# Attention and a gated feed-forward layer on one core: fewer, longer out-projection bursts in the loop, and a reordered first batch

## The chip, the core and the metric

The kernel runs on one core of a Trainium2 chip. The metric is the device time of one execution, in microseconds (us); lower is better. "Time" below is the median over executions; "span" is what the profiler saw between the first and the last instruction of one profiled execution.

Names used below: TensorE (PE) does matmuls, VectorE (DVE) and ScalarE (ACT) do elementwise work, GpSimd (POOL) does masks in the loop and issues loads. PSUM is where matmuls write. A "step" is one batch of the loop. A "pair" is two attention heads; there are four pairs (0 to 3) per batch.

## The reference

```python
# B, H, S, Nb, D = 8, 8, 576, 16, 64;  d_model = 512, d_ff = 1536
k_all = np.concatenate([beacon_k, k], axis=2)
v_all = np.concatenate([beacon_v, v], axis=2)
scores = q @ k_all.T / sqrt(D)             # causal mask; beacons always seen
a = softmax(scores)
x = (a @ v_all) as 4608 tokens x 512
out = (gelu(x @ w_gate) * (x @ w_val)) @ w_out
```

The output is 4608 x 512, float32.

## The kernel before

Scores are computed transposed, in four chunks per pair (widths 512, 480, 464 and 208 columns for each of two heads). Each chunk goes through two rotating PSUM buffers, then ScalarE's exp. A chunk therefore cannot start until the exp of the chunk two before it has been read. `ab(m)` issues chunks 0 and 1 of pair m, `cd(m)` chunks 2 and 3. `av(m)` ("attend") multiplies the exponentials by v, which gives x, and by a block of ones, which gives the denominators z. Both land in one PSUM tile `x_ps`, of which there is a single buffer; then `normalize` forms x / z. `o(n)` issues n out-projection matmuls of the batch before, which fill TensorE's time while ScalarE works. After the pairs come twelve gate/value tiles, whose first needs pair 3's product last.

```python
def normalize(b, m, by_act=False):
    ...
    if by_act:                                   # 1/z = exp(-ln z) on ScalarE
        act(ln_sb, z_ps, ACT.Ln)
        keep(nc.vector.tensor_copy(x_sb, x_ps))
        act(rec_sb, ln_sb, ACT.Exp, scale=-1.0)
    else:                                        # 1/z on VectorE
        def z_first():
            keep(nc.vector.transpose(zT_sb, z_ps))
        if m == NPAIR - 1:
            z_first()
        act(x_sb, x_ps, ACT.Copy)
        if m < NPAIR - 1:
            z_first()
        ...  # reciprocal of one column in 32, transpose back into rec_sb
    keep(nc.vector.tensor_tensor(out=xT_sb[...], in0=x_sb, in1=rec_sb, op=ALU.mult))

# batch 0: q and k of batch 0 in two groups of heads, 0-1 and 2-7
load_qk6(0, 0, 2); ...; load_qk6(0, 2, H)
# scores() of batch 0 issues its masks on VectorE right after each exp
ab(0); transpose_pe(0, 1, psum_x, "x"); cd(0)
ab(1); transpose_pe(0, 2, psum_x, "x"); cd(1)
ab(2); transpose_pe(0, 3, psum_x, "x"); cd(2)
ab(3); av(0); cd(3)
av(1, by_act=True); av(2, wide=True); av(3, by_act=True)

# batches 1 to 7
o(6); ab(0); o(8); cd(0); o(6); ab(1); o(4); av(0); cd(1); o(3)
ab(2); av(1); o(3); cd(2); o(4); ab(3); o(2); av(2); cd(3); o(5); av(3); o(7)
```

`transpose_pe` transposes q and k of the next pair on TensorE; a copy of its result on VectorE fills `qkT`, from which the scores read.

The softmax here doesn't subtract the row's maximum and nothing guards it: scores larger than these inputs give would overflow.

## Time and profile before

| | before |
|---|---|
| time, median of the first 3 runs | 411.73 us (410.74 to 412.95) |
| span of the profiled execution | 408.4 us |
| first out-projection of the loop (end of batch 0) | 60.07 us |
| one loop step, out-projection start to out-projection start | 43.29 us |
| scores of pairs 0 to 3 in batch 0 start at | 8.25, 14.26, 18.66, 23.07 us |

The first reading is where the time is. These are lines of the page of the kernel before: the chain that ended last by engine, then one of the costliest groups (line, engine, operation, output<-input, shapes, count | busy us, mean ns of one | idle us of the engine just before them and what ended it).

```profile
PE 88%; ACT 4%; DVE 4%; DMA 2%; issue 1%; POOL 1%; POOLq 0%; DVEq 0%
...
L155 PE MATMUL s_ps<-qkT 64*128 64x80 bf16 (+5 forms) x384 | 39.7, 298 | 8.6 <-DVE qkT L183 4.5
```

TensorE is 88% of the chain, so idle time on other engines mostly costs nothing. What counts is idle time on TensorE, and the group of scores (`s_ps`) has the most that something other than a load ends: 8.6 us before its matmuls.

The second reading is a piece of one loop step: the chain of waits of the kernel before in order of time (start us, length us, what).

```profile
240.43 1.58 PE x_ps L155 x36
...
242.03 0.65 ACT x_sb L158
242.68 0.84 ACT expT L158
...
243.57 0.39 PE s_ps L155 x2
...
244.36 1.56 PE x_ps L155 x36
...
246.67 0.39 PE s_ps L155 x4
```

Here the chain leaves TensorE: attend of pair 0 ends, ScalarE copies x out of PSUM (0.65 us), then does the exp of chunk 2, and only then the scores of pair 2 may start at 243.57. Each switch between scores, attend and out-projection also changes the array mode (64-row, 64-column, full). TensorE's timeline gives the length of a step, from one out-projection start to the next:

```profile
233.22 1.46 PE L155 MATMUL o_ps<-wo_sb,hT_sb 128*128 128x512 bf16 x6
...
276.51 1.46 PE L155 MATMUL o_ps<-wo_sb,hT_sb 128*128 128x512 bf16 x6
```

The third reading is batch 0: TensorE's timeline (start us, length us, engine, line, operation, output<-input, shape, count, and in brackets the idle time before and what ended it).

```profile
9.77 0.69 PE L167 MATMUL t_ps<-ident,qk_103 96*64 96x96 bf16 x12 [0.51 <-DMA qk_103<-in_q_dram]
11.91 0.69 PE L167 MATMUL t_ps<-ident,qk_103 96*64 96x96 bf16 x12 [1.45 <-DMA qk_103<-in_k_dram]
...
14.26 1.01 PE L155 MATMUL s_ps<-qkT 64*128 64x512 bf16 x8 [0.86 <-ACT expT L158]
...
18.66 1.01 PE L155 MATMUL s_ps<-qkT 64*128 64x512 bf16 x8 [1.46 <-DVE qkT L183]
...
23.07 1.01 PE L155 MATMUL s_ps<-qkT 64*128 64x512 bf16 x8 [1.46 <-DVE qkT L183]
...
36.77 0.38 PE L155 MATMUL gv_ps<-xT_sb,wg_sb 128*128 128x512 bf16 x1 [0.51 <-DVE xT_sb L303]
```

Pair 1's transposes wait for q and then for k of heads 2 to 7. Scores of pair 1 start at 14.26. Those of pairs 2 and 3 follow 4.4 us apart, each after 1.46 us of idle time that ends with the copy into `qkT`. VectorE's timeline shows why the copy is late:

```profile
16.83 0.44 DVE L224 TENSOR_TENSOR expT<-expT,tri 128x256 bf16<-128x256 bf16 x2 [0.59 <-ACT expT L158]
17.19 1.35 DVE L178 COPY qkT<-t_ps 128x1152 bf16<-128x1152 bf16 x1
```

The copy of 1.35 us stands in VectorE's queue behind two masks (16.83), and these wait for an exp.

### The profile page before, as it was taken

Reading aid. Unit: us, or ns where it says so; the run is one execution under the profiler, and the core shown is the slowest. Engines: PE = TensorE matmul, PEld = TensorE weight load, DVE = VectorE, ACT = ScalarE, POOL = GpSimd, SP = SyncE. Lnnn points to the kernel's source line nnn. Section 1 sums busy time; section 2 is a strip of 40 time slices with the busy share of each in tenths; the row PEclk is TensorE's granted clock in tenths of the full one; section 3 lists DMA queues with packets and bytes.
Section 4 is the critical chain, followed back from the end, with each engine's and each line's share of the span. In section 5 each row is a group of like instructions: output and inputs, shape, how many; then the busy total and the mean of one; then the engine's idle time right before and its main releaser. Section 6 shows DMA issues by size and latency. Waiting matters only on the chain.

```text
span 408.4 us, 7414 instructions
## 1 busy us (share of the span) xinstructions
PE 385.3 (94%) x3036; PEld 183.0 (45%) x3036; DVE 194.7 (48%) x308; ACT 209.2 (51%) x286; POOL 156.3 (38%) x275
## 2 busy tenths in 40 slices
PE   2678999999999999999999999999999999999996
PEld 1344444544444444544444445444444444444442
DVE  2456463654266426633484436532664266333332
ACT  2665328643784368535763486437833684322210
POOL 8633573591239414860469035912400141000000
PEclk9999999999999999999999999999999999999999
DMA  8999991099019960999159910993023001000012
GB/s 112 186 206 205 166 126 52 29 154 165 33 48 113 148 86 27 100 164 88 53 54 173 120 53 28 153 143 73 32 67 79 27 27 53 0 0 28 26 51 104
DMA packets 139122, 36.24 MB, mean 89 GB/s; under 512 B 126800, under 2 KB 134480, under 8 KB 139088
## 3 DMA queue, kind: packets, MB, share of 16 engines
q0 software_dynamic: 103952, 19.14, 60.7%
q1 hardware_dynamic: 35136, 16.62, 18.6%
q8 instruction: 24, 0.39, 0.4%
q14 instruction: 10, 0.08, 0.1%
HBM read 38.27 MB, written 9.44 MB: 117 GB/s over the span
## 4 chain that ended last, share of the span: by engine, by line
PE 88%; ACT 4%; DVE 4%; DMA 2%; issue 1%; POOL 1%; POOLq 0%; DVEq 0%
PE gv_ps L155 45%; PE o_ps L155 23%; PE x_ps L155 12%; PE s_ps L155 7%; ACT expT L158 3%; DMA qk_103<-in_k_dram 2%; ACT x_sb L158 1%; DVE qkT L178 1%; PE t_ps L167 1%; DVE xT_sb L303 1%; POOL qk_103 L109 0%; DVE zT_sb L289 0%; DVE x_sb L282 0%; DVE hT_sb L331 0%; ACT ge_sb L158 0%
## 5 line engine op out<-in xcount | busy, mean ns | idle before, releaser
L158 ACT ACTIVATE ge_sb<-gv_ps 128x512 bf16<-128x512 f32 x108 | 64.5, 597 | 131.9 <-PE gv_ps L155 131.9
L331 DVE TENSOR_TENSOR hT_sb<-gv_ps,ge_sb 128x512 bf16<-128x512 f32 x108 | 74.7, 692 | 116.0 <-ACT ge_sb L158 116.0
L158 ACT ACTIVATE expT<-s_ps 128x1024 bf16<-128x1024 f32 (+3 forms) x128 | 103.5, 861 | 22.0 <-PE s_ps L155 20.2
L155 PE MATMUL gv_ps<-xT_sb,wg_sb 128*128 128x512 bf16 x432 | 112.3, 379 | 2.1 <-DVE xT_sb L303 1.9
L227 POOL TENSOR_SCALAR_AFFINE_SELECT expT<-expT 128x256 bf16<-128x256 bf16 (+2 forms) x140 | 53.4, 392 | 157.7 <-ACT expT L158 157.6
L155 PE MATMUL gv_ps<-xT_sb,wv_sb 128*128 128x512 bf16 x432 | 112.2, 379 | 0.0
L155 PE MATMUL o_ps<-wo_sb,hT_sb 128*128 128x512 bf16 x432 | 107.3, 381 | 0.0
L155 PEld LDWEIGHTS <-wv_sb 128*128 128x128 bf16 x432 | 42.2, 98 | 54.6 <-issue 4.6
L155 PEld LDWEIGHTS <-wg_sb 128*128 128x128 bf16 x432 | 41.8, 98 | 50.0
L155 PEld LDWEIGHTS <-hT_sb 128*128 128x128 bf16 x432 | 37.1, 98 | 47.3 <-issue 9.4
L155 PE MATMUL s_ps<-qkT 64*128 64x80 bf16 (+5 forms) x384 | 39.7, 298 | 8.6 <-DVE qkT L183 4.5
L355 DVE COPY o_sb<-o_ps 128x512 f32<-128x512 f32 x36 | 24.8, 689 | 42.5 <-PE o_ps L155 42.5
L155 PE MATMUL x_ps<-expT,ones 128*64 128x432 bf16 (+1 forms) x558 | 42.1, 247 | 0.0
L289 DVE STREAM_TRANSPOSE zT_sb<-x_ps 128x576 f32<-128x576 f32 x29 | 22.7, 781 | 32.4 <-ACT x_sb L158 32.4
L158 ACT ACTIVATE x_sb<-x_ps 128x576 f32<-128x576 f32 x29 | 18.9, 651 | 27.4 <-DVE zT_sb L289 15.8
L155 PEld LDWEIGHTS <-qkT 64*128 64x128 bf16 x384 | 13.8, 96 | 37.2 <-issue 27.3
L303 DVE TENSOR_TENSOR xT_sb<-x_sb,rec_sb 128x576 bf16<-128x576 f32 x32 | 25.1, 784 | 1.8
L155 PEld LDWEIGHTS <-ones 128*64 128x64 bf16 (+1 forms) x578 | 23.6, 112 | 4.8 <-issue 0.2
L298 DVE STREAM_TRANSPOSE rec_sb<-r_sb 128x576 f32<-128x576 f32 x30 | 23.3, 778 | 1.0
L155 PE MATMUL x_ps<-expT,v_sb_95 128*64 128x80 bf16 (+5 forms) x270 | 22.4, 253 | 1.1 <-DVE zT_sb L289 1.0
L155 PE MATMUL x_ps<-expT,v_sb_98 128*64 128x80 bf16 (+5 forms) x288 | 22.8, 246 | 0.1
L109 POOL DMA_DIRECT2D v_sb_98<-in_v_dram x20 | 17.0, 891 | 11.0 <-DMA wv_sb<-in_moe_w_val_dram 3.7
(48 smaller groups left out, 183.8 us busy)
## 6 DMA issues: line engine op xcount, KB each, us to landing
out_dram<-o_sb SPq DMA_DIRECT2D x36, 256.0 KB, 2.0
v_sb_95<-in_v_dram POOLq DMA_DIRECT2D x12, 128.0 KB, 7.7
wg_sb<-in_moe_w_gate_dram POOLq DMA_DIRECT2D x3, 512.0 KB, 11.4
wv_sb<-in_moe_w_val_dram POOLq DMA_DIRECT2D x3, 512.0 KB, 13.2
wo_sb<-in_moe_w_out_dram POOLq DMA_DIRECT2D x1, 1536.0 KB, 23.4
v_sb_98<-in_v_dram POOLq DMA_DIRECT2D x12, 128.0 KB, 10.3
q_sb_93<-in_q_dram POOLq DMA_DIRECT2D x12, 128.0 KB, 4.4
q_sb_96<-in_q_dram POOLq DMA_DIRECT2D x12, 128.0 KB, 4.1
```

Source lines behind the costliest of these rows:

```text
L109: keep(nc.gpsimd.dma_start(out=out_ap, in_=in_ap))
L155: keep(nc.tensor.matmul(out_ap, lhsT, rhs, start=start, stop=stop, **kw))
L158: keep(nc.scalar.activation(out_ap, in_ap, func, **kw))
L167: keep(nc.tensor.transpose(out_ap, in_ap, ident[0:n, 0:n]))
L178: nc.vector.tensor_copy(qkT[:, m, :, NB:SK].rearrange("p w (t r) -> p w t r", r=6), t_ps[:, 0:2, 0:S].rearrange("p w (r t) -> p w t r", r=6),)
L227: nc.gpsimd.affine_select(out=d, in_=d, pattern=[[0, 2], [1, n]], compare_op=ALU.is_ge, fill=0.0, base=NB if t == 0 else 0, channel_multip ...
L289: keep(nc.vector.transpose(zT_sb, z_ps))
L298: nc.vector.transpose(rec_sb.rearrange("p (c o) -> p c o", o=32), r_sb.to_broadcast([P, S // 32, 32]))
L303: nc.vector.tensor_tensor(out=xT_sb[:, m, b * S : (b + 1) * S], in0=x_sb, in1=rec_sb, op=ALU.mult)
L331: nc.vector.tensor_tensor(out=h_of[ci][:, fi, :], in0=gv_ps[:, 1, :], in1=ge_sb, op=ALU.mult)
L355: keep(nc.vector.tensor_copy(o_sb[:, ti, :], o_ps))
```

## The change

It intends to switch TensorE's work less often in the loop: each of the pairs 1 to 3 has its scores, the attend of the pair before, the rest of its scores, then one out-projection burst. The last pair's product reads x straight from PSUM, without ScalarE's copy. In batch 0, the masks move behind the transpose copies, q/k are loaded in three groups of heads, and pairs 2 and 3 take 1/z by Ln and Exp and the product from PSUM.

```diff
@@ scores
-        (masks of the chunk)
+        if b:
+            masks(b, m, c)
@@ normalize
-    def normalize(b, m, by_act=False):
+    def normalize(b, m, by_act=False, direct=False):
+        x_sb = x_ps
+        if not direct:
+            x_sb = npool.tile([P, S], FP32, name="x_sb", tag="x_sb")
         if by_act:
             act(ln_sb, z_ps, ACT.Ln)
-            keep(nc.vector.tensor_copy(x_sb, x_ps))
+            if not direct:
+                keep(nc.vector.tensor_copy(x_sb, x_ps))
         else:
-            if m == NPAIR - 1:
-                z_first()
-            act(x_sb, x_ps, ACT.Copy)
-            if m < NPAIR - 1:
-                z_first()
+            if not direct:
+                act(x_sb, x_ps, ACT.Copy)
+            keep(nc.vector.transpose(zT_sb, z_ps))
@@ loads
-    load_qk6(0, 2, H)
+    load_qk6(0, 2, 4)
+    load_qk6(0, 4, H)
@@ batch 0
+            # masks of pairs 0 and 1 (chunks 0, 1) after the last transpose copy,
+            # the others ahead of av(0) and after cd(3)
-            av(2, wide=True)
-            av(3, by_act=True)
+            av(2, wide=True, by_act=True, direct=True)
+            av(3, by_act=True, direct=True)
@@ batches 1 to 7
             o(6)
             ab(0)
-            o(8); cd(0); o(6); ab(1); o(4); av(0); cd(1); o(3)
-            ab(2); av(1); o(3); cd(2); o(4); ab(3); o(2); av(2); cd(3); o(5); av(3)
+            o(10)
+            cd(0)
+            o(8)
+            for m in range(1, NPAIR):
+                ab(m)
+                av(m - 1)
+                cd(m)
+                o(6 if m < NPAIR - 1 else 5)
+            av(3, direct=True)
             o(7)
```

(Several lines are joined with semicolons, and the mask calls are shortened to a comment.)

More of the change, by code (lines that the diff above doesn't have):

```diff
@@ L215, in scores, with masks @@
         act(expT[:, :, o : o + w], s_ps[:, :, 0:w], ACT.Exp, scale=QK_SCALE)
+        if b:
+            masks(b, m, c)
+    def masks(b, m, c):
+        expT = exp_of[b * NPAIR + m]
         for t, s_lo, _, _ in CHUNKS[c]:
@@ L276, in normalize @@
         del exp_of[i]
-        x_sb = npool.tile([P, S], FP32, name="x_sb", tag="x_sb")
         rec_sb = npool.tile([P, S], FP32, name="rec_sb", tag="rec_sb")
+        x_sb = x_ps
+        if not direct:
+            x_sb = npool.tile([P, S], FP32, name="x_sb", tag="x_sb")
         if by_act:
@@ L286, in normalize @@
             r_sb = npool.tile([P, S // 32, 1], FP32, name="r_sb", tag="r_sb")
-            def z_first():
-                keep(nc.vector.transpose(zT_sb, z_ps))
-            if m == NPAIR - 1:
-                z_first()
-            act(x_sb, x_ps, ACT.Copy)
-            if m < NPAIR - 1:
-                z_first()
+            if not direct:
+                act(x_sb, x_ps, ACT.Copy)
+            keep(nc.vector.transpose(zT_sb, z_ps))
             keep(nc.vector.reciprocal(r_sb, zT_sb.rearrange("p (c o) -> p c o", o=32)[:, :, 0:1]))
@@ L394, in cd, with av @@
             scores(b, m, 3)
-        def av(m, wide=False, by_act=False):
+        def av(m, wide=False, **kw):
             for t in AV_ORDER:
                 attend(b, m, t, wide)
-            normalize(b, m, by_act)
+            normalize(b, m, **kw)
         keep(nc.scalar.preload_act_table_set(SET_EXP))
         if b == 0:
-            ab(0)
-            transpose_pe(0, 1, psum_x, "x")
-            cd(0)
-            ab(1)
-            transpose_pe(0, 2, psum_x, "x")
-            cd(1)
-            ab(2)
-            transpose_pe(0, 3, psum_x, "x")
-            cd(2)
-            ab(3)
-            av(0)
-            cd(3)
+            for m in range(NPAIR):
+                ab(m)
+                if m == NPAIR - 1:
+                    for mm_ in (0, 1, 2):
+                        for c in range(4):
+                            if (mm_, c) > (1, 1):
+                                masks(0, mm_, c)
+                    av(0)
+                    for c in (0, 1):
+                        masks(0, m, c)
+                else:
+                    transpose_pe(0, m + 1, psum_x, "x")
+                    if m == 2:
+                        for mm_, c in ((0, 0), (0, 1), (0, 2), (0, 3), (1, 0), (1, 1)):
+                            masks(0, mm_, c)
+                cd(m)
+            for c in (2, 3):
+                masks(0, NPAIR - 1, c)
             av(1, by_act=True)
-            av(2, wide=True)
-            av(3, by_act=True)
+            av(2, wide=True, by_act=True, direct=True)
+            av(3, by_act=True, direct=True)
         else:
@@ L420 @@
             ab(0)
-            o(8)
-            cd(0)
-            o(6)
-            ab(1)
-            o(4)
-            av(0)
-            cd(1)
-            o(3)
-            ab(2)
-            av(1)
-            o(3)
-            cd(2)
-            o(4)
-            ab(3)
-            o(2)
-            av(2)
-            cd(3)
-            o(5)
-            av(3)
+            o(10)
+            cd(0)
+            o(8)
+            for m in range(1, NPAIR):
+                ab(m)
+                av(m - 1)
+                cd(m)
+                o(6 if m < NPAIR - 1 else 5)
+            av(3, direct=True)
             o(7)
```

## The prediction

> **What bounds it now.** The chain of waits is 88% TensorE: 45% gate/value matmuls, 23% out-projection, 12% attend, 7% scores. From 60 us on, TensorE never idles for long, so only three things can be gained: array-mode switches, short waits, and the start.
>
> *One batch step* (timeline, 233.22 to 257.09 us, out-projection start to the first gate/value tile's last contraction slice: 23.87 us). A 512-column matmul is pitched at 0.2176 us (90 in 19.58). Six out matmuls should take 1.31 us, but take 1.39 when followed by scores; each mode change costs about 0.1 us by that arithmetic. The Trainium skill ("TensorEngine Tiling (Array Packing)", Key Properties) says that changing the tiling mode drains the array; the trace agrees with about 0.1 us. Before there are 21 mode changes per step, after it 18: 0.3 us. Waits now (timeline): second-half scores of pair 0 about 0.1 us (late exp, table load 1.28 us); scores of pair 2 wait 0.43 us on ScalarE's exp plus 0.2 inside; pair 3 about 0.25; attend of pair 3 about 0.1 on the transpose; gate/value about 0.2 on the last product.
>
> *Batch 0* (0 to 36.77 us): the q/k load of heads 2 to 7 lands at 9.77 (q) and 11.91 (k), TensorE waits 0.5 and 1.45 us. Then the pairs run 4.4 us apart (scores start 14.26, 18.66, 23.07), because the transpose copy (1.42 us with its small second part) queues on VectorE behind masks which wait for exp; scores wait 1.5 us for it each time. The tail, attend end 33.27 to 36.77, is a VectorE chain.
>
> **What the change does.** *Loop:* per pair, scores 0.53, attend 1.56, scores 0.39, out burst 1.39: 3.87 us. ScalarE per pair: exp 1.89 + 1.35, copy 0.55: about 3.7 us busy. Following buffer releases, the fourth chunk waits about 0.14 us for the second exp (the out matmuls between them are gone), giving a period near 4.02 us. The step: 6.42 before pair 1, two periods of 4.03, then 2.09 to the end of attend(2), then a VectorE chain of two normalizations, 6.35. Sum 22.9 against 23.87: about 0.95 us per step, seven steps, 6.6 us. The last product from PSUM removes a 0.65 us ScalarE copy that is off the path (it came after the transpose already): worth nothing in the loop.
>
> *Batch 0:* heads 2 and 3 (144 KB each) should land by about 8 us, so pair 1's transposes follow at once; scores of pair 1 at 12 instead of 14.26. Copies no longer behind masks: period about 3.7 instead of 4.4 us. With pair 2 by Ln/Exp and straight from PSUM, VectorE loses two transposes, and the tail after the last attend falls from 3.5 to about 2.3 us. Gate/value's last slice at 32.5 instead of 36.8: 4.3 us.
>
> **Prediction.** 411.7 - 6.6 - 4.3 = 400.8; I allow a little for new waits: 401.3 us, range 398.3 to 405.0. Faster by over 2%: 0.79; within 2%: 0.20; slower: 0.01.
>
> **Right if** the timeline shows: steps about 42.35 us apart instead of 43.3; score-to-score distance of pairs near 4.0 us in the loop; no out matmul burst split by ScalarE waits over 0.3 us; in batch 0 scores near 12, 15.7, 19.4 us and gate/value flowing by about 32.5.
>
> **Wrong if** ScalarE becomes the limit of the pair period (above 4.3 us: the loop gain vanishes); VectorE's chain behind attend(2) grows, and gate/value waits for it; delayed masks hold up attend in batch 0; TensorE stays on its slow clock longer (before 28 us the same attend takes 2.9 us, afterwards 1.6); or the later v and weight loads arrive too late.

## The result, and the profile after

| | before | after |
|---|---|---|
| time, median | 411.28 us (410.74 to 412.95, 4 runs) | 398.35 us (397.83 to 400.3, 4 runs) |
| span of the profiled execution | 408.4 us | 396.6 us |
| end of batch 0 (first out-projection) | 60.07 us | 56.23 us |
| loop step | 43.29 us | 42.18 us |
| from the last step's start to the end | 88.6 us | 87.4 us |

The ratio is 0.9688 (95% interval 0.9643 to 0.9732). Ratios here are the mean time of one kernel's fast runs over that of the other's fast runs of the same rounds, so they are not quite the ratio of the medians. A second set of the unchanged kernel after, with more rounds, gave 0.9695 (0.9667 to 0.9723).

The spans differ by 11.8 us. That splits into 3.84 us in batch 0, 6.80 us in the six distances between the starts of the seven steps, and 1.16 us in the last step: 11.8. The times differ by 12 to 13 us. The profiled execution of the kernel before took 410.45 us and so lies about 1 us below its median.

The same lines of the page, for the kernel after:

```profile
PE 92%; DVE 2%; DMA 2%; ACT 1%; POOL 1%; issue 0%; POOLq 0%
...
L155 PE MATMUL s_ps<-qkT 64*128 64x80 bf16 (+5 forms) x384 | 39.2, 297 | 4.0 <-ACT expT L158 2.5
```

The chain is 92% TensorE instead of 88%, and idle time before scores fell from 8.6 to 4.0 us; what is left is all in batch 0. The chain in the same place of a loop step:

```profile
231.28 0.53 PE s_ps L155 x8
231.81 1.56 PE x_ps L155 x36
233.36 0.54 PE s_ps L155 x4
233.90 1.40 PE o_ps L155 x6
235.30 0.53 PE s_ps L155 x8
235.83 1.56 PE x_ps L155 x36
```

ScalarE is gone from this piece of the chain. The pairs start 235.30 - 231.28 = 4.02 us apart. Chunks 2 and 3 (233.36) take 0.54 us, where the kernel before needed 0.39 (246.67): about 0.14 us of waiting for the second exp has come back here, as reckoned in the prediction. A step by TensorE's timeline, with the start of pair 1's scores between its two ends:

```profile
224.80 1.46 PE L155 MATMUL o_ps<-wo_sb,hT_sb 128*128 128x512 bf16 x6
...
231.21 0.60 PE L155 MATMUL s_ps<-qkT 64*128 64x512 bf16 x8
...
266.98 1.46 PE L155 MATMUL o_ps<-wo_sb,hT_sb 128*128 128x512 bf16 x6
```

TensorE's timeline of batch 0:

```profile
9.16 1.17 PE L167 MATMUL t_ps<-ident,qk_103 96*64 96x96 bf16 x24
...
11.99 1.01 PE L155 MATMUL s_ps<-qkT 64*128 64x512 bf16 x8 [0.83 <-ACT expT L158]
...
13.97 0.69 PE L167 MATMUL t_ps<-ident,qk_103 96*64 96x96 bf16 x12 [0.35 <-DMA qk_103<-in_k_dram]
...
16.31 1.01 PE L155 MATMUL s_ps<-qkT 64*128 64x512 bf16 x8 [0.86 <-ACT expT L158]
...
20.08 1.01 PE L155 MATMUL s_ps<-qkT 64*128 64x512 bf16 x8 [0.83 <-ACT expT L158]
...
32.93 0.38 PE L155 MATMUL gv_ps<-xT_sb,wg_sb 128*128 128x512 bf16 x1 [0.84 <-DVE xT_sb L306]
```

Scores of pair 1 start at 11.99 instead of 14.26, later pairs 3.8 to 4.3 us apart. What ends the wait now is an exp (0.83 us), no longer the copy. VectorE's queue shows copies first and the 15 masks of pairs 0 to 2 behind them:

```profile
18.59 1.36 DVE L178 COPY qkT<-t_ps 128x1152 bf16<-128x1152 bf16 x1 [2.34 <-PE t_ps L167]
...
19.93 2.90 DVE L229 TENSOR_TENSOR expT<-expT,tri 128x224 bf16<-128x224 bf16 x15
```

### The profile page after: what moved, and what is told of

It is laid out like the page before. It is cut to its first block, busy times and chain, and to the rows that moved or that the text cites. A ratio compares the mean times of both kernels' runs of the same rounds, so it can differ in the third digit from the quotient of the medians.

```text
span 396.6 us, 7393 instructions
## 1 busy us (share of the span) xinstructions
PE 380.7 (96%) x3036; PEld 185.7 (47%) x3036; DVE 190.5 (48%) x304; ACT 202.4 (51%) x280; POOL 156.5 (39%) x277
## 4 chain that ended last, share of the span: by engine, by line
PE 92%; DVE 2%; DMA 2%; ACT 1%; POOL 1%; issue 0%; POOLq 0%
PE gv_ps L155 46%; PE o_ps L155 25%; PE x_ps L155 12%; PE s_ps L155 8%; DMA qk_103<-in_k_dram 2%; PE t_ps L167 1%; POOL qk_103 L109 1%; DVE qkT L178 1%; ACT expT L158 0%; DVE xT_sb L306 0%; DVE hT_sb L334 0%; ACT ge_sb L158 0%; DVE expT L229 0%; DVE zT_sb L298 0%; DVE rec_sb L301 0%
## 5 line engine op out<-in xcount | busy, mean ns | idle before, releaser
L232 POOL TENSOR_SCALAR_AFFINE_SELECT expT<-expT 128x256 bf16<-128x256 bf16 (+2 forms) x140 | 52.5, 387 | 144.0 <-ACT expT L158 143.8
L155 PE MATMUL o_ps<-wo_sb,hT_sb 128*128 128x512 bf16 x432 | 103.6, 380 | 0.0
L155 PEld LDWEIGHTS <-hT_sb 128*128 128x128 bf16 x432 | 38.8, 98 | 46.7 <-issue 3.0
L155 PEld LDWEIGHTS <-qkT 64*128 64x128 bf16 x384 | 14.6, 96 | 30.9 <-issue 20.5
L155 PEld LDWEIGHTS <-ones 128*64 128x64 bf16 (+1 forms) x578 | 23.6, 112 | 4.8 <-issue 0.2
L109 POOL DMA_DIRECT2D v_sb_98<-in_v_dram x20 | 17.0, 876 | 12.5 <-DMA wv_sb<-in_moe_w_val_dram 3.4
L306 DVE TENSOR_TENSOR xT_sb<-x_sb,rec_sb 128x576 bf16<-128x576 f32 x23 | 17.4, 758 | 0.9
L109 POOL DMA_DIRECT2D v_sb_95<-in_v_dram x20 | 17.0, 895 | 0.6 <-issue 0.5
```

Source lines behind the costliest of these rows:

```text
L109: keep(nc.gpsimd.dma_start(out=out_ap, in_=in_ap))
L155: keep(nc.tensor.matmul(out_ap, lhsT, rhs, start=start, stop=stop, **kw))
L232: nc.gpsimd.affine_select(out=d, in_=d, pattern=[[0, 2], [1, n]], compare_op=ALU.is_ge, fill=0.0, base=NB if t == 0 else 0, channel_multip ...
L306: nc.vector.tensor_tensor(out=xT_sb[:, m, b * S : (b + 1) * S], in0=x_sb, in1=rec_sb, op=ALU.mult)
```

## The experiments

All outputs are right.

### The loop order alone

The kernel before with the new order of batches 1 to 7 and nothing else; the last pair keeps ScalarE's copy.

```diff
-            o(8); cd(0); o(6); ab(1); o(4); av(0); ...   # old order
+            o(10); cd(0); o(8)
+            for m in range(1, NPAIR): ab(m); av(m - 1); cd(m); o(6 or 5)
+            av(3); o(7)
```

> The kernel before with the new loop order alone; last product, masks and loads as before. Theory A (the order removes waits and three mode changes per step, about 1.1 us per step, independently of the rest): 7 steps x 1.1 = 7.7 us less, ratio 0.981; scores of pairs 1, 2, 3 start 4.03 us apart. Rival B (the order helps only because the last product comes straight from PSUM): under 3 us less, ratio above 0.993.

Measured: ratio 0.9786 (0.9767 to 0.9805), median 403.08 against 411.75 us; most steps 42.25 us long, 1.04 us shorter than before. So the order works by itself, and rival B falls. It is some two thirds of the whole gain.

### Batch 0 alone

The kernel after with the old loop order and the old last product.

```diff
-            (new loop order)
+            o(8); cd(0); o(6); ab(1); o(4); av(0); ...   # old order
```

> The kernel after with the old loop order (and the last product of the loop through ScalarE, as before): only batch 0 is changed. Theory A (the parts add): 3.8 us less than before, ratio 0.991, steps 43.3 us apart. Rival (the earlier start is given back when the later weight and v loads arrive late): ratio above 0.997 and a TensorE wait on a DMA or a copy around batch 1.

Measured: ratio 0.9879 (0.9859 to 0.9899), median 406.33 us. Batch 0 ended at 55.55 us in its profile, 4.5 us earlier than before, so the gain was a little above what was expected. Nothing is given back around batch 1. In later steps, however, scores waited twice for a transposing load into `qkT`, 1.3 us in all, which the profiles of before and after don't show; see the section on what stays open. Loop alone (2.1%) and batch 0 alone (1.2%) add up to 3.3%, against 3.1% together: the parts add within the intervals.

### The last product: ScalarE's copy after the transpose

The kernel after, with the last pair as in the kernel before: VectorE transposes z first, ScalarE copies x meanwhile.

```diff
-            av(3, direct=True)
+            av(3)                  # x through ScalarE's copy
+            # normalize, last pair: transpose of z first, then the copy
```

> The kernel after, but in the loop the last pair's x goes through ScalarE's copy again, after the transpose of z as in the kernel before. Theory A (that copy was off the path): the same as after within 0.7 us, ratio to before 0.969; gate/value waits for the last product as long as in after (0.1 us). Rival B (ScalarE's copy and the later table load delayed the first Gelu): 0.3 us or more per step lost, over 2 us in all.

Measured: ratio 0.9703 (0.9678 to 0.9729), median 399.31 us; undisturbed steps 42.25 us against 42.18. The copy runs beside VectorE's chain, as its line in ScalarE's timeline shows: it waits for the transpose, and the first Gelu does not wait for it.

```profile
290.65 0.65 ACT L158 ACTIVATE x_sb<-x_ps 128x576 f32<-128x576 f32 x1 [2.26 <-DVE zT_sb L299]
```

So the product from PSUM is worth 0.07 us per step against this order, 0.5 us over seven steps. That is close to nothing, as theory A said. In VectorE's timeline the last product starts 0.88 us after the start of the transpose back into `rec_sb` in this run, and 0.82 us in the kernel after.

### The last product: ScalarE's copy before the transpose

```diff
-            av(3, direct=True)
+            av(3)                  # copy first, transpose of z waits for it
```

> The kernel after, but in the loop the last pair's x goes through ScalarE's copy and the transpose of z waits for it, as for the other pairs. Theory A: VectorE's chain behind the last attend starts later: the copy would end about 0.65 us after attend(3), while VectorE is free 0.19 us after it, so about 0.5 to 0.6 us per step, of which gate/value sees nearly all (it already waits 0.1): 3.5 to 4.3 us slower than after, ratio to before about 0.979. So the worth of the product from PSUM depends on what it is compared with. Rival: no loss, VectorE's chain is not what gate/value waits for.

Measured: ratio 0.9792 (0.9774 to 0.9809), median 403.13 us; step 42.84 us, 0.66 us longer than after. VectorE's timeline around the last two pairs of a step, first of the kernel after, then of this run:

```profile
244.15 0.76 DVE L306 TENSOR_TENSOR xT_sb<-x_sb,rec_sb 128x576 bf16<-128x576 f32 x1
244.82 0.78 DVE L298 STREAM_TRANSPOSE zT_sb<-x_ps 128x576 f32<-128x576 f32 x1
...
246.75 0.76 DVE L306 TENSOR_TENSOR xT_sb<-x_ps,rec_sb 128x576 bf16<-128x576 f32 x1
```

```profile
289.04 0.76 DVE L306 TENSOR_TENSOR xT_sb<-x_sb,rec_sb 128x576 bf16<-128x576 f32 x1
290.37 0.78 DVE L298 STREAM_TRANSPOSE zT_sb<-x_ps 128x576 f32<-128x576 f32 x1 [0.57 <-ACT x_sb L158]
...
292.30 0.76 DVE L306 TENSOR_TENSOR xT_sb<-x_sb,rec_sb 128x576 bf16<-128x576 f32 x1
```

In the first, the last transpose follows the product before it at once; in the second it waits 0.57 us for ScalarE. TensorE pays for it, as its timeline of this run shows at the last contraction slice of the first gate/value tile:

```profile
293.11 0.38 PE L155 MATMUL gv_ps<-xT_sb,wg_sb 128*128 128x512 bf16 x1 [0.60 <-DVE xT_sb L306]
```

The likely reason for the wait is a shared bank; no run put x and z of a loop step in separate banks, so this is not shown. x takes columns 16 to 591 and z 592 to 1167 of one PSUM tile, so they share the bank of columns 512 to 1023. The Trainium skill ("PSUM — Partial Sum Buffer", section "PSUM bank collisions raise a hardware error") says that two engines must not use one bank and quadrant at the same time, two readers included. The trace agrees as far as the order goes: here z's transpose waits for ScalarE's copy of x, and in the run before it ScalarE's copy waited 2.26 us until the transpose was done. No run here tried both at once.

So the two runs together give the worth of the product from PSUM: 0.07 us per step where the transpose goes first, 0.66 us where the copy goes first.

### Every product of the loop from PSUM

```diff
-                av(m - 1)
+                av(m - 1, direct=True)
```

> The kernel after, with every pair's product in the loop from PSUM: ScalarE's copy (0.65 us per pair) goes, but the accumulator is held until the product, 2.6 us after z's transpose starts, instead of until the transpose is read. Theory A (a single accumulator buffer: the next attend waits): attend to attend at least 1.56 + 2.75 = 4.3 us instead of 4.03, and about 1 us before the last attend: about 1.4 us per step, 10 us slower than after, ratio to before about 0.993; TensorE waits on the product before attend. Rival B (ScalarE limits the pair period): the period falls from 4.03 to 3.88 us and it is faster than after by 2 us or so.

Measured: ratio 1.0057 (1.0042 to 1.0072), slower than the kernel before. The step is 44.10 us, 1.92 us longer than after; 1.4 were expected. The first matmuls of the attends of pairs 1, 2 and 3 in one step of TensorE's timeline, each with its wait:

```profile
244.50 0.44 PE L155 MATMUL x_ps<-expT,v_sb 128*64 128x496 bf16 x4 [0.32 <-DVE xT_sb L306]
...
248.91 0.44 PE L155 MATMUL x_ps<-expT,v_sb 128*64 128x496 bf16 x4 [0.46 <-DVE xT_sb L306]
...
253.42 0.44 PE L155 MATMUL x_ps<-expT,v_sb 128*64 128x496 bf16 x4 [1.30 <-DVE xT_sb L306]
```

Each attend now waits until the product before it has read x: 0.32 + 0.46 + 1.30 = 2.08 us in this step. From pair 0's attend (240.08) to pair 1's is 4.42 us, namely 1.57 us of attend and 2.85 us until the product is done and TensorE resumes; the expectation had put the second part at 2.75. Taking 0.65 us off ScalarE bought nothing, because the single accumulator became the limit. Rival B falls. This is why only the last pair, after which nobody needs the accumulator soon, is taken from PSUM.

### Four more mode changes per step

```diff
             o(6)
-            ab(0); o(10); cd(0); o(8)
+            scores(b, 0, 0); o(5); scores(b, 0, 1); o(5)
+            scores(b, 0, 2); o(4); scores(b, 0, 3); o(4)
```

> The kernel after, with pair 0's two score groups each split by out matmuls, o6 c0 o5 c1 o5 c2 o4 c3 o4: four more mode changes per step, same work, no wait by my reckoning of the exps. Theory A (a mode change costs about 0.1 us): 0.4 us per step, 2.8 us slower than after, ratio to before 0.976; TensorE has no new wait there. Rival B (mode changes are free, the loop gained from waits alone): same as after within 0.7 us.

Measured: ratio 0.98 (0.9785 to 0.9814); step 42.60 us, 0.42 us longer than after, or 0.105 us per mode change. The whole difference lies in the part before pair 1's scores, which takes 233.89 - 227.06 = 6.83 us here and 231.21 - 224.80 = 6.41 us in the kernel after:

```profile
227.06 1.46 PE L155 MATMUL o_ps<-wo_sb,hT_sb 128*128 128x512 bf16 x6
...
233.89 0.60 PE L155 MATMUL s_ps<-qkT 64*128 64x512 bf16 x8
```

The waits view of this run shows no TensorE wait in the loop. That view can miss a short wait inside a burst, so the bursts count too: in TensorE's timeline each added out-projection burst takes 0.2176 us per matmul and 0.1 us more, and the two halves of a score group take 0.1 us more than the whole, with nothing left over for a wait. So mode changes do cost time, while TensorE looks busy. That is what the Trainium skill ("TensorEngine Tiling (Array Packing)", Key Properties) says of changing the mode, that it drains the array; the number is from this run. The three mode changes that the change saves per step are worth 3 x 0.105 = 0.3 us of the 1.11 us. The four added here are all between scores and out-projection, those saved a mix; but in the timeline of the kernel after, a score group takes 0.52 to 0.53 us whether attend or out-projection follows, and an attend takes 1.56 to 1.57 us before either scores or out-projection. The other 0.8 us are waits: set against these undisturbed lengths, the bursts of one step hold about 1.4 us of waits in the kernel before and 0.5 us in the kernel after. Only 0.43 us of the 1.4 stand in the timeline as idle time.

### The parts of batch 0

Three runs changed the kernel before in one thing each: only the loads in three groups, only the masks moved, only the products of pairs 2 and 3.

```diff
# loads only
-    load_qk6(0, 2, H)
+    load_qk6(0, 2, 4)
+    load_qk6(0, 4, H)
# masks only: masks(0, m, c) issued where the kernel after has them
# products only
-            av(2, wide=True); av(3, by_act=True)
+            av(2, wide=True, by_act=True, direct=True); av(3, by_act=True, direct=True)
```

> The kernel before with q/k of batch 0 in three head groups, nothing else. Theory A: pair 1's transposes start at 9.2 us instead of waiting to 11.9, but its copy then queues behind pair 0's masks of the second chunk (which end at 11.25), so scores of pair 1 start near 12.7 instead of 14.26, the later pairs still 4.4 us apart: gate/value's last slice 1.5 us earlier, near 35.2. Rival (the load alone is the whole of the gain at the start): near 34, scores of pair 1 near 12.0.

> The kernel before with only the masks of batch 0 put behind the transpose copies. Theory A: scores of pair 1 stay at 14.26 us (the load is late and no mask is in the way there), but pairs 2 and 3 follow 3.75 us apart instead of 4.4: gate/value's last slice 1.3 us earlier, near 35.4. Rival (the masks only move: they delay attend of pair 0 by as much): no gain, 36.8.

> The kernel before with only pairs 2 and 3 of batch 0 changed: pair 2 by Ln/Exp, both products from PSUM. Theory A: VectorE loses two transposes, a reciprocal and a copy from the tail; attend(3) still ends near 33.3 us, gate/value's last slice at about 35.6 instead of 36.77. So 1.1 of the 3.8 us. Rival (ScalarE's four Ln/Exp in a row replace VectorE's chain as the limit): 36.3 or later.

| run | scores of pairs 1, 2, 3 start | last slice of the first gate/value tile | ratio of times (95%) |
|---|---|---|---|
| before | 14.26, 18.66, 23.07 | 36.77 | 1 |
| loads only | 12.59, 16.99, 21.39 | 34.74 | 0.998 (0.9959 to 1.0001) |
| masks only | 13.70, 17.46, 21.23 | 35.24 | 1.0003 (0.9983 to 1.0022) |
| products only | 14.67, 19.08, 23.48 | 36.00 | 0.9937 (0.9915 to 0.9959) |
| after | 11.99, 16.31, 20.08 | 32.93 | 0.9688 |

The mechanisms are as theory A said. With the loads alone, pair 1 starts 1.7 us earlier and the distance stays 4.4 us. With the masks alone, the distance falls to 3.76 us, worth 1.3 us; but 0.4 us of it is given back later, because attend of pair 3 waits for a copy of x that stands behind the late masks in VectorE's queue (0.38 us at 30.18, and the same at 29.06 in the kernel after). So one item of the prediction's "wrong if", masks that hold up attend, came true in small. With the products alone, the last slice follows pair 3's scores after 12.5 us instead of 13.7. The profiles give 2.0, 1.5 and 0.8 us, but part of that is chance. The transposes that wait for k of heads 2 to 7 start at 11.91 us in the kernel before, at 11.35 with the masks alone and at 12.32 with the products alone, where nothing in the loads had changed; and with the loads alone the first attend took 2.56 instead of 2.92 us, because TensorE left its slow rate earlier (see the closing list). Without these differences (and 0.05 us of clock with the masks alone) the three parts come to about 1.7, 0.9 and 1.2 us, an estimate from these traces. The times don't repeat either split: 0.2%, nothing and 0.6%. An interval of 0.2% is 0.8 us here, and the clock (below) moves batch 0 by about 1 us between executions, so how the gain of batch 0 divides among its three parts in ordinary executions is not settled. Their effect together is: the run of batch 0 alone measured it at 1.2%, where the three ratios add up to 0.8%.

### Two further steps

What the prediction's arithmetic still left in a step was 0.1 us of waiting for the last product. In the next run ScalarE, idle at that point, makes 1/z of the last pair by Ln and Exp. The run after it loads q/k of batch 0 in four groups as well.

```diff
-            av(3, direct=True)
+            av(3, by_act=True, direct=True)
# second run, also:
-    load_qk6(0, 4, H)
+    load_qk6(0, 4, 6)
+    load_qk6(0, 6, H)
```

> The kernel after, with the last pair of each loop step by Ln and Exp on ScalarE, which is idle there until the first Gelu, product from PSUM. Theory A: the product comes at about 2.2 instead of 2.9 us after attend(3), so gate/value's wait of 0.1 us goes: 0.7 us in all, ratio to before 0.967; the table load ends 0.7 us before the first Gelu. Rival: the table load, later by 1.4 us + 1.3, delays the first Gelu and the gate/value pipeline: slower than after by 1 us or more.

> As the run before it, and q/k of batch 0 in four head groups (2 heads each). Theory A: pair 2's transposes no longer wait 0.35 us for k of heads 4 to 7, and pair 2's scores come 3.8 instead of 4.3 us after pair 1's: another 0.5 us. Rival: the two more issues delay v and the weights, TensorE waits for them: nothing gained.

> The kernel after, unchanged, with more rounds, to put the last two runs beside it (0.9664 and 0.9653). If their 0.11 us per step and the fourth head group are real: ratio to before 0.968 to 0.970, 1 to 1.5 us above them; loop steps again 42.18 us. If they are noise: 0.966 or below. And the clock: if pair 1's attend runs at the slow rate this time (about 2.6 us instead of 1.4), gate/value's last slice comes about 13.9 us after pair 3's scores instead of 12.85.

Measured: ratios 0.9664 (0.9642 to 0.9685) and 0.9653 (0.9629 to 0.9678), and 0.9695 (0.9667 to 0.9723) for the kernel after again. Undisturbed steps are 42.07 us in both, 42.18 in the kernel after. ScalarE's timeline at the end of a step of the first shows that the table load ends before the first Gelu, so the rival falls:

```profile
246.02 0.68 ACT L158 ACTIVATE rec_sb<-ln_sb 128x576 f32<-128x576 f32 x1
246.72 1.28 ACT L441 ACT_TABLE_LOAD   x1
248.68 0.60 ACT L158 ACTIVATE ge_sb<-gv_ps 128x512 bf16<-128x512 f32 x1 [0.67 <-PE gv_ps L155]
```

With four groups, all pairs start 3.77 us apart; the kernel after had one distance of 4.32 us in one profile and 3.78 us in the other. Both versions have lower ratios than the kernel after in both of its sets, and the shorter step is plain in the trace. The intervals of the times overlap, though (0.9667 to 0.9678 for the second), so 0.2 to 0.4% over the kernel after is likely, not shown. The last run's condition on the clock did not arise: pair 1's attend ran at the fast rate (1.43 us), and the last slice came 12.88 us after pair 3's scores. In the run with the last pair by Ln and Exp, where that attend took 2.72 us, it came 13.88 us after them, as reckoned for the slow rate.

## Why the prediction was right

The range (398.3 to 405.0 us) held the measured 398.35 us by 0.05 us, far less than executions of one kernel differ (397.83 to 400.3), and that is luck; the mechanism is what the terms below confirm. 401.3 was 3 us too high (2 us against the second set's median of 399.12). Point by point:

- **The pair period in the loop** was put at 4.02 to 4.03 us, with 0.14 us of waiting for the second exp. Measured 4.02 us and 0.54 against 0.39 us. Right.
- **The part before pair 1** was put at 6.42 us, measured 231.21 - 224.80 = 6.41 us. Right.
- **From attend(2) to the first gate/value tile** was put at 6.35 us. Measured 247.56 - 241.35 = 6.21 us. This is the term of the loop that was too large. The same stretch of the kernel before took 257.09 - 250.83 = 6.26 us; the prediction put it 0.1 us higher without giving a reason, while the chain starts as before (the transpose of z begins 0.86 us after attend(2), before it was 0.85), and the product from PSUM, called worth nothing, saves 0.07 us.
- **Mode changes** at about 0.1 us, 0.3 us per step: 0.105 us measured by adding four.
- **The loop in sum**: 6.6 us predicted; seven times 1.11 us is 7.8 us in the profile, and 2.1% of 411.75, or 8.8 us, in the times of the loop alone.
- **Batch 0**: 4.3 us predicted, 3.84 us in the first profile of after, 4.5 us in that of batch 0 alone. Scores were put near 12, 15.7 and 19.4 us; measured 11.99, 16.31 and 20.08, and 11.93, 15.71 and 19.47 in the second profile. The first profile waited 0.35 us for k of heads 4 to 7, a load that the prediction had counted as early enough. The tail from attend(3)'s end to the last slice, put at 2.3 us, measured 32.93 - 30.62 = 2.31 us.
- **The allowance** of 0.5 us for new waits was not needed in the first profile; the second lost 1.2 us in two steps (next section).

The remainder is in the kernel before: its profile, from which every term was read, came from an execution of 410.45 us, while its median was 411 to 411.8 us over all sets but one. The sum of the terms therefore falls about 1 us short of the measured difference.

### What stays open

In several profiles, of kernels with the old and with the new loop, scores at the start of a step wait for a transposing load into `qkT`. This is TensorE's timeline of the second profile of the kernel after:

```profile
142.72 0.21 PE L155 MATMUL s_ps<-qkT 64*128 64x80 bf16 x2 [0.87 <-DMA qkT<-k_sb]
```

Steps that it lengthens are 0.1 to 1.4 us longer, at most three per profile and not the same ones from run to run. The first profiles of before and after had none on TensorE. What delays these loads was not tested.

## What to carry to other kernels

When TensorE looks 94% busy, count how often the kind of matmul changes: at 0.105 us each, the changes are invisible as idle time (and so were two thirds of the waits here), and one long burst of filler is better than several short ones as long as the buffers between the engines still let the next exp start. Before removing a copy out of PSUM, ask what else the copy did: here it freed the accumulator early, and the same edit was worth 0.07 us, 0.66 us or minus 1.9 us per step, depending on what followed. On a queue that runs in order, put the work that TensorE waits for ahead of the work that waits for others, as with the transpose copies and the masks.

## What the Trainium skill lacked or had wrong

- "TensorEngine Tiling (Array Packing)", Key Properties: it says that a mode change drains the array, and gives no time. Here it cost 0.105 us (0.42 us for four changes per step).
- "TensorE: Matmul & The Clock Gate", section "What's actually happening": its default slow clock, left after about 3.4 us of sustained work in a free-running window, fits what batch 0 shows, but TensorE stayed slow far longer here. It began at 4.7 us, was busy 9.0 of the 12 us from 8 to 20 us (4.1 of them transposes), and still ran at the slow rate until 23.6 us in one profile and until about 28 us in another. Pair 1's attend took 1.43 us in the kernel after and 2.72 us in the run with the last pair by Ln and Exp. It is chance and not the kernel: eight profiles have this same batch 0, and pair 1's attend took 1.43 or 1.44 us in four of them and 2.72 or 2.73 in the other four. How busy a window must be for the clock to rise was not tested here, so this does not show the page to be wrong. TensorE's timeline of the first two, pair 1's first attend group and the start of pair 2's:

```profile
25.55 0.44 PE L155 MATMUL x_ps<-expT,v_sb_95 128*64 128x496 bf16 x4 [1.17 <-DVE zT_sb L298]
...
26.98 0.41 PE L155 MATMUL xs_ps<-expT,v_sb_95 128*64 128x512 bf16 x3
```

```profile
24.71 0.69 PE L155 MATMUL x_ps<-expT,v_sb 128*64 128x496 bf16 x4 [0.89 <-DVE zT_sb L298]
...
27.43 0.67 PE L155 MATMUL xs_ps<-expT,v_sb 128*64 128x512 bf16 x4
```

  The granted-clock column showed 1.00 in both (windows view, 20 to 25 and 25 to 30 us), so in this profile the slow rate is seen only in the durations of matmuls of one shape.
- "TensorE: Matmul & The Clock Gate", section "Back-to-back issue gap": it gives about 131 ns per matmul for 512 columns in a stream of weight loads and matmuls. Here such a stream ran at 217.6 ns (90 matmuls in 19.58 us), which agrees with the page's figure for isolated matmuls (216 ns) instead.
- "ScalarE: Activation LUTs", section "What ACT_TABLE_LOAD costs": the load of 1283 ns agrees (1.28 us); the further 1.38 us of drain that it counts is not seen here. In the kernel before, a Gelu ended at 234.02 us, the load ran from 234.04 to 235.32, and the next exp began at 235.33.
- No page that I read has the price of holding the accumulator for a product from PSUM. The product itself took 757 ns with x from PSUM and 758 ns with x from SBUF (means of 8 and 23 in the kernel after).
